# Values of an attention step computed token-major, with the input stationary and the weights moving, in the steps that carry one lane

## The chip, the cores and the metric

The kernel runs on one core of a Trainium2 chip. The metric is device time in microseconds: three timed runs before the change gave 3451.55, 3455.74 and 3460.07, median 3455.74. One further execution was recorded by the hardware profiler; its span is 3448.0 us.

## The reference

A vector sequence x of 2048 tokens by 640 features goes through four layers, each on the layer norm of its input and each added to it: A, B, A, B, with the same weights both times.

```
A (recurrent memory attention), 64 segments of 32 tokens, 32 heads of 192:
    mem = mem0                                  # 8 rows of 640
    for each segment s:
        h = concat(mem, x[s])                   # 40 rows
        q, k, v = h @ Wq, h @ Wk, h @ Wv        # each 640 -> 32 x 192
        p = softmax(mask(q k^T / sqrt(192)))    # per head, 40 x 40
        o = (p v) @ Wo                          # 6144 -> 640
        mem = o[:8];  output o[8:]
B (token mixer and MLP):
    h = gelu(layernorm(x) @ w1), quarters shifted by 1 or 2 tokens, @ w2
    x1 = x + that;  output x1 + gelu(layernorm(x1) @ w3) @ w4
```

The memory makes layer A serial: a segment needs the memory rows that the segment before it put out. All matrices are bf16.

## The kernel before

**Steps and lanes.** The two A layers run side by side. Lane 0 is the first A layer, lane 1 the second, five segments behind (LAG). Step t works on segment t of lane 0 and segment t - 5 of lane 1 at once, so that one pass over the weights serves both. There are 69 steps. Steps 0 to 4 carry lane 0 alone and steps 64 to 68 carry lane 1 alone; these ten are the one-lane steps. The 59 between carry both. The input of a step is held transposed in hT, features on the partitions: per 128 features, 80 columns, of which each lane owns 40. In a two-lane step matmuls run over W = 80 columns, in a one-lane step over W = 56 (ONE, line 36).

**Work of a step.** The 32 heads are cut into eight groups of four (768 features, GW), handled as four pairs. `proj_pair` (line 546) makes k, q and v of a pair, `attend` (line 619) then does the attention of each group. For each of k, q and v and each group, line 566 issues 30 matmuls: six output chunks of 128 features by five chunks of the 640 inputs, the weights stationary and hT moving. The results are feature-major: features on partitions, tokens along the columns. Keys and queries are wanted so. Values are wanted token-major, since the product of probabilities and values (pso, line 678) takes V as its stationary operand with tokens on the partitions. So a group's values take a detour: ScalarE copies psv to vF (line 596), TensorE transposes six chunks of 128 columns into pvt (line 604), and ScalarE and VectorE copy half each into V (lines 615 and 613).

**Attention and output.** `attend` forms scores (pss, line 631), masks them and finds a shift on VectorE, takes the exponential on ScalarE and normalizes on VectorE (Pm), transposes (pst, line 664), copies to PT, multiplies with V (pso) and copies the result to oT on VectorE (line 690) and ScalarE (line 688). The output product psy (line 705) has 30 matmuls per group; one PSUM tile sums all eight groups. At the end of a step ScalarE copies the new memory columns of psy into the next step's hT (line 724), which the next keys wait for.

**Mixer.** Layer B runs in chunks (`chunk` and `chunk_end`), one every two steps, its matmuls interleaved with the attention's; the last chunk follows step 68.

**Weights.** [...] Part of each pair's weights is resident and the rest streams from HBM in every step through a ring of nine tiles (wst), issued by SyncE, whose transfers follow one order; the mixer's weights share that queue. The last pair's tiles are kept for the first pair of the next step, which runs through the pairs in the opposite direction. Wo is resident after step 0. In step 0 all resident weights are loaded.

**Order of work.** Nothing is issued in the order of the source. Each operation is handed to a planner (`Plan`, line 84) with an engine, an estimated duration, a due time and the buffers that it reads and writes. The planner places the operations on a model of the engines, choosing among those that could start by due time, and the program is written out in that order, fixed for each engine. PSUM is eight tiles of a bank each: six in pool A for attention and two in pool B for the mixer. A tile is claimed when its first operation is placed and is free after its last. V, kT, qT and Pm have one buffer each.

Of the kernel before, what the change touches and what calls it, by code (L numbers as in the profile page):

```python
# [9 lines left out]
ACT = mybir.ActivationFunctionType  # L10
# [3 lines left out]
f32 = mybir.dt.float32  # L14
# [7 lines left out]
HG = 4  # L22
STREAM = {"k": 3, "q": 3, "v": 2}
RING_A = 9
MORE = {("v", 0): -1, ("v", 3): -1, ("k", 1): 1, ("q", 1): 1, ("q", 2): 1}
RING_B = 3
STEP = 48.0
KEEP = True
WO_FROM = 1
Y_POOL = "A"  # L30
PSUM_POOLS = {"A": 6, "B": 2}
OT_BUFS = 8
KT_BUFS = 1
VT_BUFS = 1
# [17 lines left out]
LAST_PACE = 0.55  # L52
# [201 lines left out]
def kernel(  # L254
# [16 lines left out]
    nc = tc.nc  # L271
# [131 lines left out]
    def B(*key):  # L403
        key = ALIAS.get(key, key)
        if key not in bufs:
            bufs[key] = Buf()
        return bufs[key]
# [7 lines left out]
    def ps(cls, shape, dtype, name):  # L415
        b = Slotted(cls, None)

        def make():
            return psum.tile(shape, dtype, name=name, tag=f"{cls}{b.slot}")
        b.make = make  # L420
        return b

    def T(b):
        if b.obj is None:
            b.obj = b.make()
        return b.obj

    def mm_us(n, m=128, k=1):
        return k * (max(54, n) / 2400.0 + 0.0025)

    def dve_us(n, ps_=True):
        return ((120 if ps_ else 58) + n) / 960.0 + 0.02

    def act_us(n, ps_=True):
        return ((172 if ps_ else 224) + n) / 1200.0 + 0.02
# [92 lines left out]
    def attention_step(t):  # L528
# [16 lines left out]

        def proj_pair(i_, pr):
            s0 = base + sl * 2 * i_
            for kind, at in (("k", 0.0), ("q", 0.2), ("v", 0.5)):
                if i_ == 0 and t > 0 and KEEP:
                    wbs, wv = kept[kind]  # L550
                else:
                    wbs, wv = load_pair(kind, pr, s0 + at * 2 * sl, LEAD_A)
                if i_ == NPAIR - 1:
                    kept[kind] = wbs, wv
                for j in range(2):
                    G = t * NG + 2 * i_ + j
                    due = s0 + (at + 0.1 * j) * 2 * sl
                    pq = ps("A", [P, GC, NS], f32, "ps" + kind)

                    nres = KC - STREAM[kind] + MORE.get((kind, pr), 0)  # L560
# [31 lines left out]
                    else:  # L592
# [14 lines left out]
                        for hf in range(2):  # L607
                            def fe(op, pvt=pvt, V_=V_, hf=hf):
# [7 lines left out]
                            add("DVE" if hf else "ACT", 0.35 if hf else act_us(GWH), due, fe, r=(pvt,),  # L616
                                w=(B("V", G % VT_BUFS, hf),))

        def attend(p_, g):
            G = t * NG + p_  # L620
            s0 = base + sl * p_
            q, k_, V_ = qT, kT[G % KT_BUFS], Vt[G % VT_BUFS]
            pss = ps("A", [P, HG * NS], f32, "pss")
            hi = s0 + 0.5 * sl

            def fs(op):
                o = T(pss)
                seq = [(0, 1, 0, 0), (1, 1, 2, 3), (2, 1, 3, 4), (3, 1, 5, 7), (0, 2, 1, 1), (2, 2, 4, 5)]
                for n_, (i, w_, c, j) in enumerate(seq):
                    m_ = wide(c, GC - 1)  # L630
                    nc.tensor.matmul(out=o[0:m_, i * N:(i + w_) * N].rearrange("p (a b) -> p a b", a=w_),  # L631
                                     lhsT=qTw[:, c * NS:c * NS + m_], rhs=k_[:, j:j + w_, c0:c0 + N],
                                     start=(n_ == 0), stop=(n_ == len(seq) - 1), skip_group_check=True)
            add("PE", mm_us(N, N, 4) + mm_us(2 * N, N, 2), hi - 4, fs,
                r=(B("qT"), B("kT", G % KT_BUFS, 0), B("kT", G % KT_BUFS, 1), B("kT", G % KT_BUFS, 2)), w=(pss,))
            sm_ = sm[G % 2]
            Pb = Pm
            smk, Pk = B("sm", G % 2), B("P")

            def f1(op):  # L640
                o = T(pss)[0:NR, 0:HG * N].rearrange("p (a b) -> p a b", a=HG)
                nc.vector.tensor_tensor_reduce(out=o, in0=o, in1=maskt.unsqueeze(1).to_broadcast([NR, HG, N]),  # L642
                                               scale=-scale, scalar=3.0e38, op0=ALU.add, op1=ALU.min,
                                               accum_out=sm_[0:NR, 0:1])
            add("DVE", dve_us(HG * N) + 0.02, hi - 4, f1, r=(pss,), w=(pss, smk))

            def f2(op):
                o = T(pss)[0:NR, 0:HG * N].rearrange("p (a b) -> p a b", a=HG)
                nc.scalar.activation(out=Pb[0:NR, :, c0:c0 + N], in_=o, func=ACT.Exp, bias=sm_[0:NR, 0:1], scale=-1.0)  # L649
            add("ACT", act_us(HG * N) + 0.09, hi - 4, f2, r=(pss, smk), w=(Pk,))  # L650

            def f3(op):
                nc.vector.tensor_reduce(out=sm_[0:NR, 2:2 + HG], in_=Pb[0:NR, :, c0:c0 + N], axis=AX.X, op=ALU.add)
                nc.vector.reciprocal(out=sm_[0:NR, 6:6 + HG], in_=sm_[0:NR, 2:2 + HG])
                nc.vector.tensor_tensor(out=Pb[0:NR, :, c0:c0 + N], in0=Pb[0:NR, :, c0:c0 + N],
                                        in1=sm_[0:NR, 6:6 + HG].unsqueeze(2).to_broadcast([NR, HG, N]), op=ALU.mult)
            add("DVE", 0.53 + 0.0085 * N, hi - 4, f3, w=(Pk, B("sm4", G % 2)))
            pst = ps("A", [P, HG, NS], bf16, "pst")

            def f4(op):  # L660
                o = T(pst)
                for i in range(HG):
                    w_ = wide(i, HG)
                    nc.tensor.transpose(out=o[0:w_, i, :], in_=Pmw[:, i * NS:i * NS + w_], identity=ident[0:NS, 0:NS])  # L664
            add("PE", mm_us(NS, N, 4), hi - 3, f4, r=(Pk,), w=(pst,))
            Pt = PT

            def f5(op):
                nc.scalar.copy(out=Pt[:, :, 0:N], in_=T(pst)[0:NS, :, c0:c0 + N])  # L669
            add("ACT", act_us(HG * N), hi - 4, f5, r=(pst,), w=(B("PT"),))  # L670
            pso = ps("A", [P, GC, NS], f32, "pso")

            def f6(op):
                o = T(pso)
                for hf in range(2):
                    for i2, col, c, st, sp in ((0, 0, 0, True, True), (0, 128, 1, True, False), (1, 192, 1, False, True),
                                               (1, 320, 2, True, True)):
                        nc.tensor.matmul(out=o[:, 3 * hf + c, 0:N], lhsT=V_[:, VP * hf + col:VP * hf + col + P],  # L678
                                         rhs=Pt[:, 2 * hf + i2, 0:N], start=st, stop=sp)
            add("PE", mm_us(N, k=8), hi - 3, f6, r=(B("PT"), B("V", G % VT_BUFS, 0), B("V", G % VT_BUFS, 1)), w=(pso,))  # L680
            o_ = oT[G % OT_BUFS]

            oks = [B("oT", G % OT_BUFS, hf) for hf in range(2)]
            if p_ in HALVES:
                for hf in range(2):
                    def f7(op, hf=hf):
                        if hf:
                            nc.scalar.copy(out=o_[:, 3:6, off:off + N], in_=T(pso)[:, 3:6, 0:N])  # L688
                        else:
                            nc.vector.tensor_copy(out=o_[:, 0:3, off:off + N], in_=T(pso)[:, 0:3, 0:N])  # L690
                    add("ACT" if hf else "DVE", (act_us if hf else dve_us)(3 * N), hi - 4, f7, r=(pso,), w=(oks[hf],))
            else:
                def f7(op):
                    nc.vector.tensor_copy(out=o_[:, :, off:off + N], in_=T(pso)[:, :, 0:N])
                add("DVE", dve_us(GC * N), hi - 4, f7, r=(pso,), w=oks)
            due = base + STEP - 1 + 0.02 * p_ if p_ >= WO_FROM else s0 + 2.0 * sl
            wb, wo = res_tile(("o", g), [P, GC, Dm], Wo_v[:, g], base + STEP - 2 + 0.02 * p_)
            for hf in range(2):
                def f8(op, hf=hf):
                    o = T(psy)  # L700
                    for cc in range(3 * hf, 3 * hf + 3):
                        for m in range(KC):
                            st = first_wo[0]
                            first_wo[0] = False
                            nc.tensor.matmul(out=o[:, m, cw:cw + W], lhsT=wo[:, cc, m * P:(m + 1) * P],  # L705
                                             rhs=o_[:, cc, 0:W], start=st, stop=True, skip_group_check=True)
                add("PE", mm_us(W, k=3 * KC), due, f8, r=(wb, oks[hf]), a=(psy,))
# [4 lines left out]
            attend(2 * i_, 2 * pr)  # L712
            attend(2 * i_ + 1, 2 * pr + 1)

        due = base + STEP - 5
        hn = hT[(t + 1) % 4]
        mk = B("hT", (t + 1) % 4, "m")
        take = [l for l in nxt if t + 1 - l * LAG > 0]
# [152 lines left out]
    def chunk(c):  # L871
        last = c == NCH - 1
        base = (T_A if last else 2 * c + 2) * STEP
        D = lambda x: base + x * STEP * (LAST_PACE if last else 1.0)
        PB = "A" if last else "B"
        xk, uk, vk, vxk, vTk = B("xw"), B("uw"), B("vb"), B("vx"), B("vT")
        ps1 = ps(PB, [XB, KC, P], bf16, "psx")
# [262 lines left out]
    def chunk_end(c):  # L1140
        last = c == NCH - 1
        base = (T_A if last else 2 * c + 2) * STEP
        D = lambda x: base + x * STEP * (LAST_PACE if last else 1.0)
        PB = "A" if last else "B"
        xk, vxk = B("xw"), B("vx2")
        s4k = B("st", 3)
# [175 lines left out]
```

## Time and profile before

| | |
|---|---|
| timed runs, median | 3455.74 us (3451.55 to 3460.07) |
| profiled span | 3448.0 us |
| TensorE matmuls (PE) | 3308.9 us busy, 84571 instructions |
| TensorE weight loads (PEld) | 3223.3 us busy, 84573 instructions |
| VectorE | 2380.2 us |
| ScalarE | 1704.4 us |
| HBM read | 817.14 MB |
| step 0 | 88.85 us |
| steps 1 to 4 | 187.26 us |
| 59 two-lane steps, 5 to 63 | 2915.59 us |
| steps 64 to 68 | 226.60 us |
| last chunk of the mixer | 29.70 us |

Busy time counts a matmul from its start to an estimated end, and matmuls overlap in the pipeline, so a busy TensorE need not be at its peak. A step is taken to end when the copy of its memory columns starts (step 68 when the copy to yTB starts). Where a line shows a number in brackets after an operation, it is the time for which the engine stood idle before it, and the arrow names what ended that; "issue" stands for nothing that the profile shows. The granted clock is the share of TensorE's full speed that the chip let through.

### The profile page before, as it was taken

The page shows a single profiled execution, that of the slowest core. Times are in us where ns is not written, and L with a number is a line of the kernel's source. Part 1 is how long each engine was busy: PE and PEld are TensorE (multiplying, and loading weights), DVE is VectorE, ACT ScalarE, POOL GpSimd, SP SyncE. Part 2 cuts the span into 40 slices and gives each one's busy share as a digit, 9 for nine tenths or more (in the row PEclk, how much of TensorE's full clock was granted, in tenths as well). Part 3 has the DMA queues.
Part 4 walks back from the last instruction along what each step waited for, and adds up shares of the span by engine and source line. Part 5 has one row for each costly group of instructions (what it writes and reads, how often), then busy time and mean ns, then how long its engine had stood idle before and what let it go on. Part 6 is the DMA issues. An engine that isn't in the chain of part 4 may idle for free.

```text
span 3448.0 us, 187550 instructions
## 1 busy us (share of the span) xinstructions
PE 3308.9 (96%) x84571; PEld 3223.3 (93%) x84573; DVE 2380.2 (69%) x7359; ACT 1704.4 (49%) x4125; POOL 237.3 (7%) x488
## 2 busy tenths in 40 slices
PE   6889999999999999999999999999999999999887
PEld 5889999999999999999999999999999999999886
DVE  2556677777777777777767777777777777777664
ACT  2344455555555555555555555554555555555443
POOL 1000000000000000000000000000000000000000
PEclk7999999999999999999999999999999999999999
DMA  9776677667766776677668666776686667667775
GB/s 373 240 249 235 223 255 248 224 224 257 247 229 224 265 245 221 226 262 245 223 225 273 235 220 232 261 240 224 234 274 227 224 229 263 226 223 252 271 248 184
DMA packets 409757, 834.55 MB, mean 242 GB/s; under 512 B 39633, under 2 KB 207264, under 8 KB 408953
## 3 DMA queue, kind: packets, MB, share of 16 engines
q1 hardware_dynamic: 401656, 809.47, 69.0%
q8 instruction: 661, 10.83, 1.3%
q0 software_dynamic: 7136, 13.00, 1.1%
q14 instruction: 144, 1.17, 0.1%
q10 hardware_dynamic: 160, 0.08, 0.0%
HBM read 817.14 MB, written 5.24 MB: 239 GB/s over the span
## 4 chain that ended last, share of the span: by engine, by line
PE 92%; DMA 3%; issue 2%; DVE 1%; ACT 1%; SPq 1%; POOL 0%; POOLq 0%; ACTq 0%; DVEq 0%
PE psy L705 17%; PE psq L566 16%; PE psv L566 16%; PE psk L566 16%; PE pvt L604 5%; PE pso L678 4%; PE pss L631 4%; PE psh L1116 3%; PE y L1161 3%; PE pst L664 2%; PE psh L994 1%; PE hs L1053 1%; DMA wst<-in_A_Wk_dram 1%; DMA wst<-in_A_Wv_dram 1%; ACT V L615 1%
## 5 line engine op out<-in xcount | busy, mean ns | idle before, releaser
L566 PEld LDWEIGHTS <-wst 128*128 128x128 bf16 x25668 | 1039.4, 99 | 33.4 <-issue 21.6
L705 PE MATMUL psy<-oT,wo 128*128 128x80 bf16 (+1 forms) x16560 | 667.0, 200 | 23.5 <-issue 10.0
L705 PEld LDWEIGHTS <-wo 128*128 128x128 bf16 x16560 | 619.1, 100 | 27.2 <-issue 19.6
L690 DVE CAST oT<-pso 128x240 bf16<-128x240 f32 (+1 forms) x552 | 214.6, 389 | 354.2 <-ACT oT L688 342.6
L576 ACT CAST qT<-psq 128x480 bf16<-128x480 f32 (+1 forms) x552 | 292.2, 529 | 318.7 <-PE psq L566 308.9
L566 PE MATMUL psk<-hT,wst 128*128 128x80 bf16 (+1 forms) x9108 | 431.2, 200 | 9.2 <-issue 7.2
L566 PE MATMUL psq<-hT,wst 128*128 128x80 bf16 (+1 forms) x8280 | 403.1, 200 | 8.8 <-issue 7.9
L566 PE MATMUL psv<-hT,wst 128*128 128x80 bf16 (+1 forms) x8280 | 399.2, 200 | 7.3 <-issue 5.1
L566 PE MATMUL psq<-hT,wq 128*128 128x80 bf16 (+1 forms) x8280 | 379.2, 200 | 17.4 <-issue 6.5
L566 PE MATMUL psv<-hT,wv 128*128 128x80 bf16 (+1 forms) x8280 | 378.5, 200 | 9.5 <-issue 7.7
L688 ACT CAST oT<-pso 128x240 bf16<-128x240 f32 (+1 forms) x552 | 190.2, 345 | 392.5 <-PE pso L678 366.7
L615 ACT COPY V<-pvt 80x384 bf16<-80x384 bf16 x552 | 262.1, 475 | 239.3 <-PE pvt L604 218.6
L649 ACT ACTIVATE Pm<-pss,sm 80x320 bf16<-80x320 f32 (+2 forms) x552 | 279.9, 507 | 182.3 <-DVE sm L642 182.1
L566 PE MATMUL psk<-hT,wk 128*128 128x80 bf16 (+1 forms) x7452 | 348.5, 200 | 14.3 <-ACT hT L724 10.8
L566 PEld LDWEIGHTS <-wq 128*128 128x128 bf16 x8280 | 329.1, 100 | 24.9 <-issue 17.6
L590 DVE CAST kT<-psk 64x160 bf16<-64x160 f32 (+1 forms) x1104 | 336.5, 305 | 14.5
L566 PEld LDWEIGHTS <-wv 128*128 128x128 bf16 x8280 | 329.4, 99 | 15.2 <-issue 8.6
L596 ACT CAST vF<-psv 128x480 bf16<-128x480 f32 (+1 forms) x552 | 290.7, 527 | 95.1 <-PE psv L566 90.0
L642 DVE CUSTOM_DVE_ANT_1 pss<-pss,mask 80x320 f32<-80x320 f32 (+2 forms) x552 | 252.4, 476 | 105.8 <-PE pss L631 101.8
L566 PEld LDWEIGHTS <-wk 128*128 128x128 bf16 x7452 | 299.6, 100 | 23.1 <-issue 21.0
L669 ACT COPY PT<-pst 80x320 bf16<-80x320 bf16 (+1 forms) x552 | 222.7, 403 | 196.1 <-PE pst L664 192.3
L613 DVE COPY V<-pvt 80x384 bf16<-80x384 bf16 x552 | 193.6, 351 | 182.4 <-ACT V L615 101.5
(140 smaller groups left out, 4590.6 us busy)
## 6 DMA issues: line engine op xcount, KB each, us to landing
wst<-in_A_Wk_dram SPq DMA_DIRECT2D x555, 384.0 KB, 5.2
wst<-in_A_Wq_dram SPq DMA_DIRECT2D x486, 384.0 KB, 5.2
wst<-in_A_Wv_dram SPq DMA_DIRECT2D x486, 384.0 KB, 5.3
wstB<-in_B_w_dram SPq DMA_DIRECT2D x495, 320.0 KB, 4.8
wstB<-in_B_w_dram SPq DMA_DIRECT2D x132, 160.0 KB, 4.5
wo<-in_A_Wo_dram SPq DMA_DIRECT2D x8, 960.0 KB, 12.6
xw<-in_A_x_dram POOLq DMA_DIRECT2D x31, 80.0 KB, 5.1
x2d<-vbg POOLq DMA_DIRECT2D x31, 80.0 KB, 4.9
```

The costliest lines, as they stand in the source:

```text
L566: nc.tensor.matmul(out=o[:, cc, 0:W], lhsT=wv(kc, GW * j + cc * P, GW * j + (cc + 1) * P), rhs=h[:, kc, cw:cw + W], start=(kc == 0 and cc ...
L576: nc.scalar.copy(out=q[:, :, c0:c0 + N], in_=T(pq)[:, :, off:off + N])
L590: nc.vector.tensor_copy(out=k4[r0:r1, :, jj, c0:c0 + N], in_=p4[r0:r1, :, 1, off:off + N])
L596: nc.scalar.copy(out=vF[:, :, c0:c0 + N], in_=T(pq)[:, :, off:off + N])
L613: nc.vector.tensor_copy(out=dst, in_=src)
L615: nc.scalar.copy(out=dst, in_=src)
L642: nc.vector.tensor_tensor_reduce(out=o, in0=o, in1=maskt.unsqueeze(1).to_broadcast([NR, HG, N]), scale=-scale, scalar=3.0e38, op0=ALU.add, ...
L649: nc.scalar.activation(out=Pb[0:NR, :, c0:c0 + N], in_=o, func=ACT.Exp, bias=sm_[0:NR, 0:1], scale=-1.0)
L669: nc.scalar.copy(out=Pt[:, :, 0:N], in_=T(pst)[0:NS, :, c0:c0 + N])
L688: nc.scalar.copy(out=o_[:, 3:6, off:off + N], in_=T(pso)[:, 3:6, 0:N])
L690: nc.vector.tensor_copy(out=o_[:, 0:3, off:off + N], in_=T(pso)[:, 0:3, 0:N])
L705: nc.tensor.matmul(out=o[:, m, cw:cw + W], lhsT=wo[:, cc, m * P:(m + 1) * P], rhs=o_[:, cc, 0:W], start=st, stop=True, skip_group_check=True)
```

## The change

In one-lane steps `proj_pair` hands the values of all four pairs to a new function, `values`. It computes them token-major at once. The input hT (128 features by 80 columns) is the stationary operand and the weights move, 384 columns at a time. For a group there are two halves of 384 values, each a sum over the five input chunks: ten matmuls instead of 30, into two PSUM tiles of 80 rows by 384 fp32. The copy to vF and the six transposes fall away; ScalarE copies the first half straight to V and VectorE the second. All 80 rows are computed, the lane's own 40 are used. The four PSUM tiles of a pair come from pool A. Two-lane steps keep the old code. Several numbers of the due times become named constants with the values they had.

```diff
@@ -25,8 +25,17 @@
 MORE = {("v", 0): -1, ("v", 3): -1, ("k", 1): 1, ("q", 1): 1, ("q", 2): 1}
 RING_B = 3
 STEP = 48.0
+V_ONE = (0, 1, 2, 3)
+V_ON = ("ACT", "DVE")
+V_PARTS = (range(0, 5),)
 KEEP = True
 WO_FROM = 1
+AT = (0.0, 0.2, 0.5)
+AT_J = 0.1
+HI = (4.0, 3.0, 0.5)
+MIX = (0.0, 1.0)
+EARLY = 2.0
+FM = 5.0
 Y_POOL = "A"
 PSUM_POOLS = {"A": 6, "B": 2}
...
@@ -545,16 +554,19 @@
 
         def proj_pair(i_, pr):
             s0 = base + sl * 2 * i_
-            for kind, at in (("k", 0.0), ("q", 0.2), ("v", 0.5)):
+            for kind, at in zip("kqv", AT):
                 if i_ == 0 and t > 0 and KEEP:
                     wbs, wv = kept[kind]
                 else:
                     wbs, wv = load_pair(kind, pr, s0 + at * 2 * sl, LEAD_A)
                 if i_ == NPAIR - 1:
                     kept[kind] = wbs, wv
+                if kind == "v" and not both and i_ in V_ONE:
+                    values(i_, pr, s0 + at * 2 * sl, wbs, wv)
+                    continue
                 for j in range(2):
                     G = t * NG + 2 * i_ + j
-                    due = s0 + (at + 0.1 * j) * 2 * sl
+                    due = s0 + (at + AT_J * j) * 2 * sl
...
 
+        def values(i_, pr, s0, wbs, wv):
+            nres = KC - STREAM["v"] + MORE.get(("v", pr), 0)
+            pv = [[ps("A", [NS, GWH], f32, "psv") for _ in range(2)] for _ in range(2)]
+            for j in range(2):
+                for hf in range(2):
+                    for kcs in V_PARTS:
+                        def fv(op, j=j, hf=hf, kcs=kcs):
+                            a = GW * j + GWH * hf
+                            for kc in kcs:
+                                nc.tensor.matmul(out=T(pv[j][hf])[:], lhsT=h[:, kc, :], rhs=wv(kc, a, a + GWH),
+                                                 start=(kc == 0), stop=(kc == KC - 1))
+                        rb = [wbs[0]] if kcs[0] < nres else []
+                        rb += [wbs[1 + kc - nres] for kc in kcs if kc >= nres]
+                        add("PE", mm_us(GWH, k=len(kcs)), s0 + (0.2 * j + 0.05 * hf) * sl, fv,
+                            r=(*rb, *hk), a=(pv[j][hf],))
+            for j in range(2):
+                V_ = Vt[(t * NG + 2 * i_ + j) % VT_BUFS]
+                for hf in range(2):
+                    def fe(op, j=j, hf=hf, V_=V_):
+                        v0 = hf * (VP - 64)
+                        dst = V_[:, v0:v0 + 512].rearrange("n (a b) -> n a b", a=2)[:, :, 64 * hf:64 * hf + Dh]
+                        src = T(pv[j][hf])[:].rearrange("n (a b) -> n a b", a=2)
+                        if V_ON[hf] == "DVE":
+                            nc.vector.tensor_copy(out=dst, in_=src)
+                        else:
+                            nc.scalar.copy(out=dst, in_=src)
+                    add(V_ON[hf], dve_us(GWH) if V_ON[hf] == "DVE" else act_us(GWH), s0 + 0.2 * sl * j, fe, r=(pv[j][hf],),
+                        w=(B("V", (t * NG + 2 * i_ + j) % VT_BUFS, hf),))
+
...
-            hi = s0 + 0.5 * sl
+            hi = s0 + HI[2] * sl
...
-            add("PE", mm_us(N, N, 4) + mm_us(2 * N, N, 2), hi - 4, fs,
+            add("PE", mm_us(N, N, 4) + mm_us(2 * N, N, 2), hi - HI[0], fs,
...
-            due = base + STEP - 1 + 0.02 * p_ if p_ >= WO_FROM else s0 + 2.0 * sl
+            due = base + STEP - 1 + 0.02 * p_ if p_ >= WO_FROM else s0 + EARLY * sl
...
-        due = base + STEP - 5
+        due = base + STEP - FM
...
-        D = lambda x: base + x * STEP * (LAST_PACE if last else 1.0)
+        D = lambda x: base + (x * LAST_PACE if last else MIX[0] + x * MIX[1]) * STEP
```

More of the change, by code (lines that the diff above doesn't have):

```diff
@@ L644, in f1 @@
                                                accum_out=sm_[0:NR, 0:1])
-            add("DVE", dve_us(HG * N) + 0.02, hi - 4, f1, r=(pss,), w=(pss, smk))
+            add("DVE", dve_us(HG * N) + 0.02, hi - HI[0], f1, r=(pss,), w=(pss, smk))
             def f2(op):
@@ L649, in f2 @@
                 nc.scalar.activation(out=Pb[0:NR, :, c0:c0 + N], in_=o, func=ACT.Exp, bias=sm_[0:NR, 0:1], scale=-1.0)
-            add("ACT", act_us(HG * N) + 0.09, hi - 4, f2, r=(pss, smk), w=(Pk,))
+            add("ACT", act_us(HG * N) + 0.09, hi - HI[0], f2, r=(pss, smk), w=(Pk,))
             def f3(op):
@@ L656, in f3 @@
                                         in1=sm_[0:NR, 6:6 + HG].unsqueeze(2).to_broadcast([NR, HG, N]), op=ALU.mult)
-            add("DVE", 0.53 + 0.0085 * N, hi - 4, f3, w=(Pk, B("sm4", G % 2)))
+            add("DVE", 0.53 + 0.0085 * N, hi - HI[0], f3, w=(Pk, B("sm4", G % 2)))
             pst = ps("A", [P, HG, NS], bf16, "pst")
@@ L664, in f4 @@
                     nc.tensor.transpose(out=o[0:w_, i, :], in_=Pmw[:, i * NS:i * NS + w_], identity=ident[0:NS, 0:NS])
-            add("PE", mm_us(NS, N, 4), hi - 3, f4, r=(Pk,), w=(pst,))
+            add("PE", mm_us(NS, N, 4), hi - HI[1], f4, r=(Pk,), w=(pst,))
             Pt = PT
@@ L669, in f5 @@
                 nc.scalar.copy(out=Pt[:, :, 0:N], in_=T(pst)[0:NS, :, c0:c0 + N])
-            add("ACT", act_us(HG * N), hi - 4, f5, r=(pst,), w=(B("PT"),))
+            add("ACT", act_us(HG * N), hi - HI[0], f5, r=(pst,), w=(B("PT"),))
             pso = ps("A", [P, GC, NS], f32, "pso")
@@ L679, in f6 @@
                                          rhs=Pt[:, 2 * hf + i2, 0:N], start=st, stop=sp)
-            add("PE", mm_us(N, k=8), hi - 3, f6, r=(B("PT"), B("V", G % VT_BUFS, 0), B("V", G % VT_BUFS, 1)), w=(pso,))
+            add("PE", mm_us(N, k=8), hi - HI[1], f6, r=(B("PT"), B("V", G % VT_BUFS, 0), B("V", G % VT_BUFS, 1)), w=(pso,))
             o_ = oT[G % OT_BUFS]
@@ L690, in f7 @@
                             nc.vector.tensor_copy(out=o_[:, 0:3, off:off + N], in_=T(pso)[:, 0:3, 0:N])
-                    add("ACT" if hf else "DVE", (act_us if hf else dve_us)(3 * N), hi - 4, f7, r=(pso,), w=(oks[hf],))
+                    add("ACT" if hf else "DVE", (act_us if hf else dve_us)(3 * N), hi - HI[0], f7, r=(pso,), w=(oks[hf],))
             else:
@@ L694, in f7 @@
                     nc.vector.tensor_copy(out=o_[:, :, off:off + N], in_=T(pso)[:, :, 0:N])
-                add("DVE", dve_us(GC * N), hi - 4, f7, r=(pso,), w=oks)
-            due = base + STEP - 1 + 0.02 * p_ if p_ >= WO_FROM else s0 + 2.0 * sl
+                add("DVE", dve_us(GC * N), hi - HI[0], f7, r=(pso,), w=oks)
+            due = base + STEP - 1 + 0.02 * p_ if p_ >= WO_FROM else s0 + EARLY * sl
             wb, wo = res_tile(("o", g), [P, GC, Dm], Wo_v[:, g], base + STEP - 2 + 0.02 * p_)
@@ L1142, in chunk_end @@
         base = (T_A if last else 2 * c + 2) * STEP
-        D = lambda x: base + x * STEP * (LAST_PACE if last else 1.0)
+        D = lambda x: base + (x * LAST_PACE if last else MIX[0] + x * MIX[1]) * STEP
         PB = "A" if last else "B"
```

## The prediction

> **What bounds the kernel now.** I read four views in this order: the trace cut at the ends of the steps, the waits of TensorE inside the one-lane steps, the timeline of one such step, and the DMA queues. The cuts are the copies of the memory columns (line 724), one per step. Columns: stretch and its length, then busy time and count on PE, PEld, DVE, ACT and POOL, the granted clock, DMA share, GB/s.
> ```profile
> 0.00:88.85 88.85, 55.11 (x1162) 49.30 (x1163) 24.09 (x101) 18.28 (x55) 9.28 (x27) 0.74 1.00 369
> 88.85:133.50 44.65, 37.02 (x1152) 35.76 (x1152) 19.74 (x81) 15.67 (x49) 0.00 (x0) 0.92 0.58 197
> ...
> 180.19:227.45 47.26, 39.81 (x1196) 37.53 (x1194) 24.19 (x94) 18.48 (x58) 2.83 (x5) 0.96 0.76 257
> ...
> 276.11:3191.70 2915.59, 2881.88 (x72333) 2823.93 (x72331) 2103.80 (x6300) 1510.07 (x3536) 204.57 (x411) 1.00 0.71 239
> ...
> 3375.99:3418.30 42.31, 34.51 (x1152) 33.02 (x1151) 19.41 (x81) 15.77 (x49) 0.21 (x1) 1.00 0.89 297
> ```
> Step 0 is bound by DMA (share 1.00). The 59 two-lane steps are bound by TensorE (2881.88 of 2915.59). The nine other one-lane steps (1 to 4 and 64 to 68) take 187.26 + 226.60 = 413.9 us; TensorE idles about 7 us in each, although DVE, ACT and DMA are far from full. The change works there, so the question is what that idle time is:
> ```profile
> PE psq L566 <- issue: 7.0, 6, 2.0
> PE psy L705 <- issue: 6.8, 6, 2.1
> PE psk L566 <- issue: 3.1, 3, 2.0
> PE psy L705 <- DVE oT L690: 3.1, 7, 0.7
> PE pso L678 <- ACT V L615: 3.0, 4, 1.0
> ```
> These are the waits in steps 1 to 4 (total us, times, longest). Most is "issue": no semaphore explains it. The timeline of step 1 shows its rhythm:
> ```profile
> 109.62 0.57 PE L566 MATMUL psq<-hT,wq 128*128 128x56 bf16 x16
> 111.38 0.21 PE L566 MATMUL psq<-hT,wq 128*128 128x56 bf16 x2 [1.19 <-issue]
> ...
> 116.48 0.31 PE L664 MATMUL pst<-ident,Pm 80*128 80x80 bf16 x4 [1.32 <-DVE V L613]
> ...
> 119.96 0.65 PE L566 MATMUL psq<-hT,wst 128*128 128x56 bf16 x19
> 121.86 0.29 PE L566 MATMUL psq<-hT,wst 128*128 128x56 bf16 x5 [1.25 <-issue]
> ```
> From 111.38 to the pause before 116.48, and from there to the one before 121.86, the rows hold 128 matmuls each, that is 256 instructions with their weight loads. The pause put down to a value copy falls on the same count. And the page says
> ```profile
> q8 instruction: 661, 10.83, 1.3%
> ```
> These are packets, MB and share of DMA time. 661 x 256 is 169216; TensorE's matmuls and weight loads on the page are 84571 + 84573. So TensorE waits for its own instructions, fetched in blocks of 256. I cut its instructions in the nine steps at this count: 85 blocks, 46 begin with a pause over 0.3 us, 52.6 us in all (24.4 in steps 1 to 4, 28.2 in 64 to 68). A block that ended in a pause lasted 3.7 to 6.45 us with it (mean 5.06); without it, about 3.8. All 46 lie in the first 78% of their step (66 blocks, 0.80 us each); the 20 in the rest have none. The DMA row of step 3, in 40 slices, agrees:
> ```profile
> DMA  8599999999999999999999999996879600000000
> ```
> Weights stream for 80% of a step and delay the fetch, and then stop.
>
> [...] 60 key matmuls of 56 columns take 1.54 us (180.44 to 181.98), 25.7 ns each. [...]
>
> **The change, part by part, against the profiled span of 3448.0 us.** The timed runs (median 3455.74) stand 7.7 above it, and I move that median by the sum.
> 1. *TensorE work.* Per group now: 30 matmuls of 56 columns, 0.77 us, and six 128-column transposes, 0.33 us (185.15 to 185.48): 1.10. Then: ten matmuls of 384 columns. The nearest row is the 320-column one of line 1161: four took 0.54 us (194.32 to 194.86), 135 ns each; in proportion 162 ns[...]. So 1.62 us, +0.52 a group, x 8 x 9 = **+37 us**. The weight loads of 80 columns lie beside them.
> 2. *Instruction fetch.* A pair of groups issues 104 fewer instructions: 4160 of 169148 over ten steps. More important is how long a block lasts. I laid blocks of 256 on the new order of instructions: about 70 in the nine steps. 35 hold 15 to 20 of a pair's 20 value matmuls and last some 6.4 us, about as long as the longest fetch seen (6.45), so their pauses go. 34 hold none or nearly none and stay at 3.9. Of these 15 lie in the quiet end of the step and 19 before it. 19 x 0.80 = 15 us stay of 52.6: **-37 us**. Both ends: if all 34 waited to the mean 5.06, 34 x 1.2 = 41 stay (-12); if nearly none waits, -48.
> 3. *Waits at the end of a step.* pso waits for V after the chain vF copy, transpose, V copy: 3.7 us over the nine steps with the DVE share; psy waits for oT: 3.1 + 3.7. In the new order the value matmuls of the last groups stand well before their pso, and 30 to 45 psy matmuls (0.8 to 1.2 us) follow the first of the two pso, where 15 did. **-8 us** (0 to -10); the hT copy's wait of 0.3 at each step start stays.
> 4. *Clock.* Clock shares below 1.00 make 14 us of lost pulses in the nine steps. Six half-speed stretches of 3.4 us follow long pauses, 1.7 us each; about half should go: **-5 us** (0 to -8).
> 5. *ACT and DVE.* Per group ACT loses the vF copy (355 ns) and keeps a V copy (475). DVE's V copy reads fp32 and goes from 351 to an estimated 520, by the slope between the oT copies (120 columns 283, 240 columns 389). Over a step -2.8 and +1.3 us, beside TensorE on engines with at most 31 us busy of 47: 0.
> 6. *Step 0.* Extra TensorE work, partly at half clock, about +1 to +3 us a pair, but each pair is followed by a wait for wq (1.2 to 2.2 us), and the end is the last of eight Wo loads:
> ```profile
> 84.53 1.58 PE L705 MATMUL psy<-oT,wo 128*128 128x56 bf16 x30 [1.11 <-DMA wo<-in_A_Wo_dram]
> 87.23 1.58 PE L705 MATMUL psy<-oT,wo 128*128 128x56 bf16 x30 [1.12 <-DMA wo<-in_A_Wo_dram]
> ```
> TensorE would start the last 180 psy matmuls at about 75.5 and need 9.3 us, done before the last load lands at 87.2. 0 (to +3).
> 7. *Moves.* Value weights are freed later, by one pair's extra 1.0 us; SP's queue of weight loads is reordered only in the one-lane steps, and POOL's by two swaps. Behind a weight load on SP's queue stand the mixer's weights, and no wait of TensorE for those stands in its list. Two-lane order on TensorE is the same but for the first dozens of rows, and the final 29.7 us are untouched. 0 (±3). The other new constants (AT, HI, MIX, EARLY, FM and so on) repeat the numbers they replace: 0.
> 8. *PSUM.* A pair holds four of pool A's six slots at once, psy a fifth, where values and transposes held two or three. V has one buffer, so the second group's two slots stay taken until the first pso; psk, psq or pss behind them would wait. The order leaves three slots at that point, so I take 0 (to +15, 0.4 us in each of 36 pairs).
> Sum: 37 - 37 - 8 - 5 = **-13 us**, 3443.
>
> **The rivals.** *Fetches decide, and they stay (slower):* the fetch takes as long as the DMA lets it. If every one of the 34 short blocks waits to 5.06 us, 41 of 52.6 us stay, the clock gains nothing, and 37 - 12 - 8 gives +17: 3473. It decides from about 30 us of remaining pauses. For it: pauses up to 2.2 us exist. Against: no pause in the quiet end. *Nothing measurable:* matmuls and fetches cancel, and the step-end waits move elsewhere (PSUM slots, oT): 37 - 37 - 2 = -2, 3454. For it: two terms of 37 decide by their difference. *More:* with fewer pauses TensorE never outruns the fetch, 37 - 48 - 10 - 8 = -29: 3427. Against: blocks of k and q alone remain at 3.3 us.
>
> **How the numbers follow.** Forecast (gain of 10 to 22 us) 0.48, more 0.10, nothing measurable 0.27, slower 0.15. A measurement of this kernel can tell about 0.3%, 10.4 us, from no change. Part of the forecast's band falls short of it only by error of the difference: faster 0.57, same 0.28, slower 0.15. The forecast alone spans 3433 to 3446; the range that holds 8 in 10 takes in most of the others, 3423 to 3468.
>
> **What would show it.** Right: value rows of 162 ns in one-lane steps; steps of about 44.5 us, not 46; pauses at multiples of 256 down to about 15 us, and none in blocks with values; two-lane steps still 49.4; step 0 ending near 88.9. Wrong: pauses of over 30 us, value matmuls over 170 ns, new waits of psk, psq or pss for copies of V, or step 0 longer than 92.

## The result and the profile after

The changed kernel takes 3434.62 us (median of four runs, 3433.5 to 3439.02) against 3457.88 for the kernel before (the three runs named above and a fourth of 3460.02): ratio 0.9938, 95% interval 0.9921 to 0.9955. It is faster by 23 us, where the prediction said 13. Here and below the ratio is the one on record with its interval; it is not the quotient of the two medians (0.9933 here), and where the two disagree I go by the interval.

The same cut by steps as before shows where. Columns as before: stretch and length, busy time of PE, PEld, DVE, ACT and POOL, clock, DMA share, GB/s.

```profile
0.00:88.93 88.93, 54.96 (x954) 42.91 (x955) 25.70 (x101) 15.91 (x47) 9.26 (x27) 0.82 1.00 368
88.93:129.68 40.75, 37.83 (x944) 33.62 (x944) 20.92 (x81) 13.28 (x41) 0.00 (x0) 0.97 0.63 215
...
173.70:219.48 45.78, 42.28 (x1008) 36.87 (x1006) 25.66 (x94) 16.04 (x49) 2.80 (x5) 1.00 0.76 265
...
262.25:3188.11 2925.86, 2884.78 (x72353) 2825.32 (x72351) 2102.79 (x6300) 1509.84 (x3536) 204.34 (x411) 1.00 0.71 238
...
3363.75:3406.43 42.68, 38.40 (x944) 33.07 (x943) 21.09 (x81) 13.75 (x41) 0.20 (x1) 0.96 0.86 298
```

Step 0 is as long as before (88.93 against 88.85). Steps 1 to 4 take 173.32 us instead of 187.26 and steps 64 to 68 take 218.32 instead of 226.60: together 22.2 us less. That is nearly all of what the timed runs gained. The two-lane steps, whose order of matmuls on TensorE changed only in the first 650 of some 72,300, took 2925.86 us in this execution and 2915.59 in the one profiled before, and the last chunk of the mixer 30.77 and 29.70. That is why the two profiled spans, 3437.2 and 3448.0, differ by only half of what the timed runs differ by. The last section has the two-lane steps of all profiled executions; they spread by 16 us, and by 13 among the four kernels in which this order is one and the same.

The page's count of instruction blocks (packets, MB, share of DMA time), and the waits of TensorE in steps 1 to 4 of the changed kernel (total us, times, longest):

```profile
q8 instruction: 645, 10.57, 1.2%
```

```profile
PE psq L578 <- issue: 2.2, 2, 1.6
PE psk L578 <- issue: 2.1, 1, 2.1
PE psh L1157 <- DMA wstB<-in_B_w_dram: 1.3, 1, 1.3
PE psk L578 <- ACT hT L765: 0.8, 3, 0.3
PE psy L746 <- DVE oT L731: 0.8, 3, 0.3
```

Sixteen blocks fewer are fetched; 645 x 256 is 165120, and the page counts 82491 + 82493 instructions on TensorE. The "issue" waits have shrunk, the wait of pso for V is gone, and the one of psy for oT is down from 3.1 to 0.8.

For what follows I use one count, taken from each trace in the same way. In the nine one-lane steps after step 0, a gap of more than 0.25 us between the starts of two TensorE instructions is called a *pause* when it falls on the 256-instruction mark, and an *other wait* when it falls elsewhere. Value matmuls that follow each other at half clock start 0.32 us apart; such a gap counts as neither. The half-speed stretches of the clock, times one half, are the *lost clock*.

| nine steps, us | length | pauses | other waits | lost clock |
|---|---|---|---|---|
| before | 413.9 | 52.6 | 24.8 | 13.0 |
| changed | 391.6 | 19.0 | 8.4 | 3.1 |

The expectations below were written with the gaps at half clock still among the other waits of the changed kernel, where they came to 11.9.

### The profile page after: what moved, and what is told of

Its sections match the earlier page's. It is cut to its first block, busy times and chain, and to the rows that moved or that the text cites. A ratio compares the mean times of both kernels' runs of the same rounds, so it can differ in the third digit from the quotient of the medians.

```text
span 3437.2 us, 183284 instructions
## 1 busy us (share of the span) xinstructions
PE 3329.6 (97%) x82491; PEld 3207.2 (93%) x82493; DVE 2393.9 (70%) x7359; ACT 1680.8 (49%) x4045; POOL 237.0 (7%) x488
## 4 chain that ended last, share of the span: by engine, by line
PE 93%; DMA 3%; issue 2%; ACT 1%; DVE 1%; SPq 1%; POOL 0%; POOLq 0%; ACTq 0%
PE psq L578 17%; PE psy L746 16%; PE psk L578 16%; PE psv L578 15%; PE pvt L616 5%; PE pso L719 4%; PE pss L672 4%; PE psh L1157 3%; PE psv L640 3%; PE y L1202 3%; PE pst L705 2%; PE psh L1035 1%; PE hs L1094 1%; DMA wst<-in_A_Wq_dram 1%; PE psv L808 1%
## 5 line engine op out<-in xcount | busy, mean ns | idle before, releaser
L578 PEld LDWEIGHTS <-wst 128*128 128x128 bf16 x24468 | 992.8, 99 | 20.8 <-issue 10.4
L746 PE MATMUL psy<-oT,wo 128*128 128x80 bf16 (+1 forms) x16560 | 660.1, 200 | 12.9 <-DMA wo<-in_A_Wo_dram 8.2
L578 PE MATMUL psv<-hT,wst 128*128 128x80 bf16 x7080 | 348.0, 202 | 3.8 <-issue 3.7
L578 PE MATMUL psv<-hT,wv 128*128 128x80 bf16 x7080 | 333.1, 202 | 4.2 <-issue 4.0
L627 ACT COPY V<-pvt 80x384 bf16<-80x384 bf16 x472 | 224.2, 475 | 191.5 <-PE pvt L616 174.1
L578 PEld LDWEIGHTS <-wv 128*128 128x128 bf16 x7080 | 291.2, 100 | 9.6 <-issue 4.9
L608 ACT CAST vF<-psv 128x480 bf16<-128x480 f32 x472 | 262.2, 556 | 71.5 <-PE psv L578 66.4
L596 DVE CAST kT<-psk 128x320 bf16<-128x320 f32 (+1 forms) x552 | 254.7, 461 | 59.0 <-PE psk L578 52.2
```

Source lines behind the costliest of these rows:

```text
L578: nc.tensor.matmul(out=o[:, cc, 0:W], lhsT=wv(kc, GW * j + cc * P, GW * j + (cc + 1) * P), rhs=h[:, kc, cw:cw + W], start=(kc == 0 and cc ...
L596: nc.vector.tensor_copy(out=k4[:, :, 0::3, c0:c0 + N], in_=p4[:, :, 0::2, off:off + N])
L608: nc.scalar.copy(out=vF[:, :, c0:c0 + N], in_=T(pq)[:, :, off:off + N])
L627: nc.scalar.copy(out=dst, in_=src)
```

## Experiments

**Is a pause an instruction fetch behind the weight transfers?** Two kernels, one from each side, in which every streamed weight tile of the one-lane steps after step 0 (`thin`) loads a quarter of its columns. The matmuls read those in place of their own, so these kernels leave out the true weights there:

```diff
-                nc.sync.dma_start(out=T(b)[:, 0:PW], in_=w_src[kind][:, kc, cols])
+                n_ = GWH if thin else PW
+                nc.sync.dma_start(out=T(b)[:, 0:n_], in_=w_src[kind][:, kc, PW * pr:PW * pr + n_])
...
+            if thin:
+                return T(slots[kc - nres])[:, c0 % GWH:c0 % GWH + c1 - c0]
             return T(slots[kc - nres])[:, c0:c1]
```

> The kernel before, except that in steps 1 to 4 and 64 to 68 every streamed weight tile loads only 384 of its 1536 columns and the matmuls read those in place of their own; the results of these steps leave out the true weights. Instructions, their order and their count stay. Theory F (the pauses are TensorE's own instruction blocks, held up behind the weight transfers): with a quarter of the streamed bytes the fetch comes in time; pauses at the 256 count fall from 52.6 us to under 10, the clock regains about 10 us, the time falls by about 50 us to near 3408. Rival L (TensorE simply can't issue 56-column matmuls faster, or the pauses are something else than a fetch): pauses stay over 40 us, time within 10 us of before.

Measured: 3402.73 us, ratio to before 0.985 (0.9836 to 0.9865), 54 us faster. The traffic in steps 1 to 4 shows in the DMA rows, first of the kernel before, then of the thin one:

```profile
DMA packets 19998, 43.59 MB, mean 233 GB/s; under 512 B 1935, under 2 KB 8641, under 8 KB 19953
```

```profile
DMA packets 19961, 17.62 MB, mean 110 GB/s; under 512 B 1934, under 2 KB 19868, under 8 KB 19916
```

The number of packets is nearly the same, the bytes are 40%. The waits of TensorE in those steps are then

```profile
PE psy L749 <- DVE oT L734: 3.1, 7, 0.7
PE pso L722 <- ACT V L630: 3.0, 4, 1.0
PE psy L749 <- issue: 1.8, 3, 0.9
```

The two semaphore waits are those of before to the digit, while "issue" fell from some 18 us to 1.8. Pauses in the nine steps: 52.6 to 5.9 us; lost clock: 13.0 to 1.2. The TensorE instructions of both traces stand in the same order; only the traffic is less: the pauses are fetches held up by transfers. The packets of the instruction queue show where. Each brings one block. From the entry of a block to the start of the packet for the next, the median in the nine steps was 2.0 us before and 0.9 us in the thin kernel; from that start to the first instruction of the new block, at a pause, it was 2.4 us in both. So the traffic delays the start of the packet; whether a queue or the memory holds it back is not shown. Theory F stands; rival L falls.

> The changed kernel with the same quarter-width streamed loads in steps 1 to 4 and 64 to 68 (so the true weights are left out there). Theory F: with no fetch to hide, the 37 us of longer value matmuls are paid and only the 9 us of step-end waits come back; slower than the thin kernel before by about 25 us, near 3433, so the sign of the change turns. Rival L (long matmuls without the transposes are faster in themselves): 15 to 25 us faster than the thin kernel before.

Measured: 3408.28 us, ratio to before 0.9867 (0.9852 to 0.9881), which is 5.6 us slower than the thin kernel before. The sign turned, as theory F said; rival L (15 to 25 us faster) falls. But I expected 25. The nine steps differ by 11.5 us (357.2 and 368.7), and the count says why: pauses went from 5.9 to 0, and other waits from 23.1 to 6.0, twice what I had set for them. 37 - 6 - 17 = 14. In the two profiled executions the two-lane steps and the rest went the other way by 5 us, which leaves 6 between the spans, as between the timed runs. All that is left of waits in steps 1 to 4 is

```profile
PE psk L581 <- ACT hT L768: 0.8, 3, 0.3
PE psy L749 <- DVE oT L734: 0.8, 3, 0.3
```

So this kernel without traffic also measures the third term of the prediction by itself: it was too small.

**Is it the length of a block that counts, or the shorter path of V?** The changed kernel with each value matmul cut in four:

```diff
-                                nc.tensor.matmul(out=T(pv[j][hf])[:], lhsT=h[:, kc, :], rhs=wv(kc, a, a + GWH),
-                                                 start=(kc == 0), stop=(kc == KC - 1))
+                                for u in range(0, GWH, 96):
+                                    nc.tensor.matmul(out=T(pv[j][hf])[:, u:u + 96], lhsT=h[:, kc, :], rhs=wv(kc, a + u, a + u + 96),
+                                                     start=(kc == 0 and u == 0), stop=(kc == KC - 1), skip_group_check=True)
```

> The changed kernel with each 384-column value matmul cut into four of 96 columns with their own weight loads; sums, order, copies and waits as in the changed kernel. TensorE's columns stay [...], but a block of 256 instructions now passes in about 4.4 us on average. Theory F: pauses rise from 17 to about 39 us, some clock is lost, time near 3465, all of the gain gone. Rival V (the gain is the shorter path of V: no vF copy, no transposes, fewer waits): +5 us, near 3440.

Measured: 3467.52 us, ratio to before 1.0031 (1.0017 to 1.0045); theory F said 3465. Pauses are back at 42.3 us, and other waits stay low, at 6.0. The waits in steps 1 to 4 show it among the value matmuls themselves:

```profile
PE psv L641 <- issue: 5.5, 4, 1.6
PE psq L578 <- issue: 5.1, 5, 2.1
PE pso L720 <- issue: 2.3, 2, 1.6
PE psy L747 <- issue: 1.6, 1, 1.6
PE psk L578 <- ACT hT L766: 0.8, 3, 0.3
```

The path of V is the short one here, and all columns are the same; the number of instructions is different, and with it the TensorE work by about 5 us (four matmuls of 96 columns start 43 ns apart, 171 ns together, where one of 384 takes 163). Those 5 us are the small part: a gain of 23 us has become a loss of 10, and of the 27 us by which the nine steps grew (391.6 to 419.0) pauses make up 23. Rival V falls.

**Does the pause depend on the pace of issue?** The kernel before with slower matmuls in one-lane steps:

```diff
-ONE = 56
+ONE = 80
...
-                        add("PE", mm_us(W, k=GC * len(kcs)), due + 0.01 * kcs[0], fn, r=(wb, *hk), a=(pq,))
+                        add("PE", mm_us(W if both else 56, k=GC * len(kcs)), due + 0.01 * kcs[0], fn, r=(wb, *hk), a=(pq,))
```

(and so at the Wo product)

> The kernel before with the one-lane matmuls over 80 columns where they had 56 (the planner's durations and with them the order kept). Count of instructions and waits as before; only the pace changes, 35.8 ns a matmul as in two-lane steps: +86 us of TensorE time in the nine steps. Theory F: blocks of 256 pass in about 4.8 us, pauses fall from 52.6 to about 16 us, the clock regains about 10: near +40 us, 3498. Rival P (each fetch costs its pause whatever the pace): +86 us, 3544.

Measured: 3479.77 us, ratio to before 1.0074 (1.0059 to 1.0089), 23 us slower. Rival P (+86) falls. The 86 rests on the two-lane steps of the kernel before, where 12 psq matmuls over 80 columns take 0.43 us (1001.12 to 1001.55), 35.8 ns each, against 25.7 over 56. Theory F's +40 was too high, since it left 16 us of pauses and took the other waits to stay; pauses fell to 6.3, and no clock was lost. With other waits at 17.8, which is 7 less: 86 - 46 - 13 - 7 = +20, and the nine steps are 23.1 us longer. Work of 86 us on TensorE costs 23, because most of it lies in time in which TensorE would have waited for instructions.

**Which pairs bring what?** The changed code for the last pair of a step alone (`V_ONE = (3,)`) and for the first three alone (`V_ONE = (0, 1, 2)`):

> The changed values code for the last pair of a one-lane step only; the other three pairs as before. Theory S (of the change's parts, the waits at the end of a step belong to the last pair alone): TensorE +9 us, pauses for instructions 52.6 to about 49, waits other than these 25 to about 15, clock -2: near -7 us against before, 3450. Rival F-only (pauses carry the whole gain): +9 - 4 - 1 = +4 us, 3461.

Measured: 3454.23 us beside 3461.11, ratio 0.9991 (0.9979 to 1.0003): by the timed runs not to be told from no change. The interval is -7 to +1 us; it takes in theory S's -7 and leaves out F-only's +4. The trace is clearer: the nine steps take 407.3 us, 6.6 less; other waits fell from 24.8 to 12.2, pauses only from 52.6 to 51.1. The end of step 1 shows how. Before (start, length, engine and line, operation, idle time in brackets):

```profile
128.06 0.50 PE L604 MATMUL pvt<-ident,vF 128*128 128x128 bf16 x6
128.39 0.31 PE L664 MATMUL pst<-ident,Pm 80*128 80x80 bf16 x4
129.18 0.66 PE L678 MATMUL pso<-PT,V 80*128 80x40 bf16 x8 [0.47 <-ACT V L615]
130.50 0.55 PE L705 MATMUL psy<-oT,wo 128*128 128x56 bf16 x15 [0.67 <-DVE oT L690]
130.88 0.36 PE L678 MATMUL pso<-PT,V 80*128 80x40 bf16 x8
```

and in the changed kernel:

```profile
125.88 0.56 PE L746 MATMUL psy<-oT,wo 128*128 128x56 bf16 x15
126.28 0.36 PE L719 MATMUL pso<-PT,V 80*128 80x40 bf16 x8
126.48 1.37 PE L746 MATMUL psy<-oT,wo 128*128 128x56 bf16 x45
127.69 0.36 PE L719 MATMUL pso<-PT,V 80*128 80x40 bf16 x8
127.89 0.55 PE L746 MATMUL psy<-oT,wo 128*128 128x56 bf16 x15
```

V is ready when pso comes, and 45 psy matmuls stand between the two pso where oT had to be waited for.

> The changed values code for the first three pairs of a one-lane step; the last pair as before. Theory S: TensorE +28 us, pauses 52.6 to about 22, other waits 25 to about 22, clock -8: near -14 us against before, 3443; with the last pair alone it adds up to the whole change. Rival F-only: the whole gain but for the last pair's pauses, -19 us or better, 3438.

Measured: 3438.83 us, ratio 0.9951 (0.9933 to 0.9968). Nine steps: 396.1 us, 17.8 less; pauses 22.5, other waits 17.2, lost clock 5.0. The two parts add up to 24.4 us, the whole change made 22.2. Theory S fits: the last pair brings the waits, the first three bring the pauses and the clock. F-only's time for the first three (3438) is no worse a fit, but its +4 for the last pair alone misses both the timed interval and the nine steps' -6.6.

**Can the remaining pauses be had as well?** Four versions of the changed kernel. First, the value sums spread wide:

```diff
-                        add("PE", mm_us(GWH, k=len(kcs)), s0 + (0.2 * j + 0.05 * hf) * sl, fv,
+                        add("PE", mm_us(GWH, k=len(kcs)), s0 + (1.4 * j + 0.7 * hf) * sl, fv,
```

> The changed kernel with the due times of a pair's four value sums spread wide (1.4 of a group's slot between the two groups, 0.7 between the halves, where 0.2 and 0.05 stood), so that they lie between the k and q of the next pair. Blocks of 256 instructions under 4 us fall from 25 to 10 of 71. Theory F: pauses 19 to about 13 us, clock -1, near -7 us against the changed kernel, 3428. Rival: the values now come late for their pso and the waits take it back, 3435 or more.

Measured: 3463.69 us, ratio to before 1.0012 (1.0001 to 1.0022). Pauses fell to 3.3 us, more than expected, and other waits rose to 45.5. Steps 1 to 4:

```profile
PE psy L746 <- DVE oT L731: 3.6, 7, 0.7
PE pst L705 <- DVE Pm L696: 3.1, 4, 0.9
PE pso L719 <- DVE V L654: 2.2, 4, 0.6
```

With the values moved away, nothing stands between the scores and pst while VectorE and ScalarE do the softmax, and V comes late for pso. A wait took the place of the pause.

Second, `RATE_ONE = 300.0e3` where 400.0e3 stood:

> The changed kernel with the planner's rate for weight transfers in steps that carry one lane lowered from 400 to 300 GB/s, which spreads the paced loads over the step (and moves the planned order). Theory F: fewer transfers stand ahead of a fetch; pauses 19 to about 10 us, near -8 us, 3427. Rival: the loads come late and TensorE waits for weights; +5 us or more, 3440.

Measured: 3467.63 us, ratio 1.0024 (1.0014 to 1.0034). Pauses 1.8 us, other waits 51.1. Steps 1 to 4:

```profile
PE pst L705 <- DVE Pm L696: 5.3, 5, 1.7
PE psk L578 <- DMA wst<-in_A_Wk_dram: 3.2, 2, 2.7
```

The loads come late, and the moved order leaves pst bare. Third and fourth, milder steps in the same two directions: 1.0 for the second group's values in the first three pairs only, and a rate of 360.

> The changed kernel with the second group's values due later (1.0 of a slot in place of 0.2) in the first three pairs alone; the last pair as in the changed kernel. If the waits of the wide spread came from the last pair's values, they stay near 12 us here and pauses fall by a few, 19 to about 17: -2 us against the changed kernel. Rival: a later V makes pso and pst wait in every pair, +5 us or more.

Measured: 3440.18 us, ratio 0.9947 (0.9931 to 0.9963); pauses 18.8, other waits 13.5. The pauses stayed and the waits rose by 5; the nine steps, at 396.0 us, are 4.4 longer than those of the changed kernel. That is the way of the rival, though the timed runs cannot tell it.

> The changed kernel with the planner's rate for weight transfers in one-lane steps at 360 GB/s where 400 stood and 300 was slower. If pauses fall with the rate before the waits for weights begin: pauses 19 to about 14, waits near 14, -3 us. Rival: the moved order costs as much as it saves or more, 0 to +10 us.

Measured: 3433.61 us, ratio 0.9939 (0.9918 to 0.9960); pauses 14.1, other waits 11.1: a gain of 5 us against a loss of 3. By the timed runs neither can be told from the changed kernel's 0.9938. No version here beats it.

## Why the prediction was right, and where it was small

The sign, the mechanism and the place were right: one-lane steps alone, by fewer and longer instructions that let the fetch keep up. The forecast was -13 us, with a band of 10 to 22 of gain; the nine steps made -22.2, at the band's edge. Two terms of the sum were too small, and both came out beyond the ranges stated for them. By the prediction's own steps:

1. *TensorE work, +37.* The estimate of 162 ns is right. Five value matmuls take 0.81 us (95.42 to 96.23), 162 to 163 ns each:
```profile
95.42 0.49 PE L640 MATMUL psv<-wv,hT 128*80 128x384 bf16 x2
95.75 0.65 PE L640 MATMUL psv<-wst,hT 128*80 128x384 bf16 x3
96.23 0.49 PE L640 MATMUL psv<-wv,hT 128*80 128x384 bf16 x2
```
2. *Fetch, -37.* Right in the sum: pauses 52.6 to 19.0, -34, where 15 us were to stay. Right too in which blocks go: of the 31 blocks with 15 or more value matmuls none ended in a pause, of 29 with at most two 15 did. But the 15 take 18.7 us, 1.25 each, where 19 were to take 0.80 each. Fewer pauses and longer ones partly cancelled, so the close sum owes something to luck. The 0.80 came from a reading that was not quite right: in the kernel before, six of the 46 pauses come after 78% of their step, the last at 87%, so the end of a step was not free of them. The thin kernels, the split and the slower pace each moved the pauses the way that this step needs. One pause of those left shows the kind of block: it holds a single value matmul, and none is among the rows before the pause.
```profile
118.07 0.32 PE L578 MATMUL psq<-hT,wst 128*128 128x56 bf16 x6
118.22 0.23 PE L719 MATMUL pso<-PT,V 80*128 80x40 bf16 x3
119.18 0.29 PE L719 MATMUL pso<-PT,V 80*128 80x40 bf16 x5 [0.72 <-issue]
```
3. *Waits at the end of a step, -8 (0 to -10).* Too small: -16. The two waits that I listed, for V and oT, fell from 10.7 to 1.9 us, about as said. But all other waits together fell by 16 (24.8 to 8.4), and by 17 (23.1 to 6.0) where less traffic disturbs them. I had summed the two lines of the list and left the shorter waits, such as the 0.8 us of pso for PT in steps 64 to 68, uncounted.
4. *Clock, -5 (0 to -8).* Too small: 13.0 to 3.1, -10. In seven of the nine steps before, the granted clock was 0.92 to 0.98; in the changed kernel it is 0.97 and 0.96 in two and 1.00 in the rest. I let half of the half-speed stretches go. One was left inside the nine steps, besides the one that runs over from step 0. Long pauses became rare: 11 lasted 1.5 us or more before, 4 do now. Six of the 11 were followed by a half-speed stretch and one of the 4, so some of this saving may be chance. A seventh stretch, in step 1 before, followed the waits at the end of that step and went with them; it was not in my six.
5. *ACT and DVE, 0.* Right. The ScalarE copy stayed at 475 ns, the VectorE copy takes 553 (estimated 520), and no wait for it stands in the changed kernel's list.
6. *Step 0 and moves, 0.* Right for step 0: 88.93 us. One wait for a weight of the mixer (psh for wstB, 1.3 us, once) is new, where I had counted on none.
7. *PSUM, 0.* Right: no wait of psk or psq for a copy of V appears in the list. In the thin changed kernel all other waits come to 6.0 us over 36 pairs, 0.17 each, against 0.4 for the bad case.

With the TensorE work at its estimate and the other terms as measured, 37 - 34 - 16 - 10 = -23, beside -22.2 for the nine steps. The rival *more* had the right side of the size with the wrong split: it let nearly all pauses go, and 19 us stayed. The rival in which fetches stay is what the split kernel came to: +10 us.

## What to carry to other kernels

When an engine idles for no semaphore, count its instructions from one pause to the next. A fixed count, 256 here, pointed to a wait for its own program, and the packets of the instruction queue confirmed it: 661 x 256 = 169216 beside 169144 instructions. Then a term of work can be wholly or partly free if it makes blocks of instructions last longer: with 86 us more of matmul time the kernel of pace80 took 23 us more. In these runs such work paid only while the fetch was slow; with the traffic gone, the same change cost 5.6 us. And a pause removed by moving work is only a gain if that work was not filling another wait: in spread the pauses went from 19.0 to 3.3 us and the other waits from 8.4 to 45.5.

## What the runs showed of the hardware that I had not expected

In the kernel before, the pauses between one block of instructions and the next came to 52.6 of 413.9 us in the nine one-lane steps. There, the start of the packet was followed by the next instruction after 2.2 to 2.8 us at nearly every pause (3.25 at the longest). The rest of the delay, up to 4.1 us, lay between the entry of the block ahead and the start of the packet.

The two-lane steps have such pauses too, and the profiled executions differ in them. The 59 two-lane steps, in one execution of each of the twelve kernels, whose TensorE order there is the same but for at most the first 650 matmuls:

| | pauses in steps 5 to 63, us | steps 5 to 63, us |
|---|---|---|
| rate360 | 20.5 | 2914.8 |
| before | 22.7 | 2915.6 |
| v012 | 23.5 | 2918.0 |
| split4 | 27.1 | 2921.2 |
| thin_after | 27.6 | 2920.8 |
| rate300 | 28.5 | 2922.0 |
| spread | 28.9 | 2927.3 |
| pace80 | 31.5 | 2922.2 |
| changed | 33.8 | 2925.9 |
| thin_before | 34.2 | 2925.5 |
| v3 | 35.4 | 2928.9 |
| hybrid | 38.2 | 2931.1 |

From the first row to the last, 18 us more of pauses go with 16 us more of time, though not in every row in order. It is not where the blocks fall: before, thin_before and pace80 have the same order and the same count of instructions up to step 5, so the same blocks, and 22.7, 34.2 and 31.5 us of pauses. No kernel was profiled twice, so chance between executions is what is left rather than shown; the timed runs of one kernel spread as widely (3449.46 to 3465.94 in eleven runs of the kernel before). Two profiled spans of this kernel should not be compared without their stretches.
